# Experts taken by falling token count, with 448 to 384 columns, and an attention loop and tail arranged anew

## The chip, the core and the metric

The kernel runs on one core of a Trainium2 chip. A core has TensorE for matrix products, VectorE, ScalarE and GpSimd for work on elements, and SyncE, which issues most of the transfers between main memory and the core's memory (SBUF); products land in PSUM, an accumulator memory of eight banks. The engines run side by side, each through its own list of instructions in order, and wait for each other by semaphores. In the profile they are PE, DVE, ACT, POOL and SP; PEld is the loading of weights into TensorE. The metric is the time of one execution on the device, in us. The rows of a trace come from one profiled execution.

## The reference, cut to what matters

```python
def attn(q, k, v, f_logit):              # 4 batches, 8 heads, 768 tokens, 48 wide
    f = 1 / (1 + exp(-f_logit))
    for t in range(768):                 # a state of 48x48 for each batch and head
        state = f[t][:, None] * state + outer(k[t], v[t])
        y[t] = q[t] @ state
def moe(x, emb, tau, w1, w2):            # x = y as 3072 tokens of 384; 8 experts, hidden 1024
    logits = normed(x) @ normed(emb).T / tau
    e = argmax(logits); g = softmax(logits)[e]
    out[token] = g * relu(x[token] @ w1[e]) @ w2[e]
def moe2(x, w_a, w_b, w_out):            # sister: 384 -> 1536 -> 384
    return ((x @ w_a) * (x @ w_b)) @ w_out
result = moe2(moe(attn(q, k, v, f_logit)))
```

## The kernel before

All work is cut so that TensorE has products of 128 rows. Products that need the accuracy of float32 are made of three matmuls each, of a high and a low half (the names end in h and l).

**Attention.** 24 groups g (6 chunks of 128 tokens for each of 4 batches), one loop over g with the stages of several groups interleaved by hand. For each g: ScalarE makes the gate F with a tanh and then `F*0.5+0.5` (gate_f, three groups ahead). VectorE makes Bt, a running product of F, with a scan whose second operand `pat` says where it starts anew, then the reciprocal `patr`, and then Rt, a second scan over F and patr (scan_b, scan_r); `qc = q*Rt` (q_scale), and GpSimd `kt = k*Bt`. TensorE multiplies qc and kt (scores, tile pp), ScalarE, VectorE and GpSimd mask the product (pm; GpSimd's share is an affine select), TensorE forms y from pm and v and from the state S, and turns y to tokens (x_ps). VectorE updates S. Scan patterns and gates lie in SBUF. After groups 4, 8, 12, 16, 20 and 23 the tokens are routed (route, a generator that tick moves on): VectorE finds each token's expert from logits (mx, z, eq, m, oh), TensorE counts places (rk), VectorE makes the slot (pz, posi), and GpSimd scatters the token's row to a table `slots` in main memory, one transfer for each 128 tokens (scatter_row).

**Tail of attention.** The first EN = 224 tokens of expert 0 are computed early, beside the last routing (early_turn, early_h, early_split, early_y, late_turn), with weights w made from raw by w_hi and w_lo. Near its end the matmuls `pc` bring the token counts (run, run_e) and the least gate product (amp) to one row, pcs.

**Experts.** The tokens of expert e are CAP = 448 rows of `slots` (expert 0 has 224 left here). rows_load loads them, x_turn transposes them by TensorE (tile pt), and 8 steps s follow: h_part, 9 matmuls ph with the columns of all tokens, then y_part, 9 matmuls po. hh and hl are the two halves of relu(ph), made by ScalarE and VectorE; y_part of a step runs behind h_part of the next. At the end of an expert po is copied to yT at an offset off, a register read from the counts, so that rows of the next expert overwrite what is not filled. w_load and w_more bring the weights in 32 pieces of 768 KB, two of w1 and two of w2 for each expert, with a fixed order. If an expert has more tokens than CAP, a flag sends the kernel through a slower general path.

**Sister.** 72 steps of 18 matmuls with 512 columns and 12 with 384 (L1088 on), then the rows are scattered to the output.

Of the kernel before, what the change touches and what calls it, by code (L numbers as in the profile page):

```python
# [43 lines left out]
EN = 224  # L44
C0 = 2.0 ** -15


def build(tc, I, out, dbg=None):
# [28 lines left out]
    off_f = epool.tile([1, 4, NE], F32, name="off_f")  # L77
    fl2 = epool.tile([1, 4], F32, name="fl2")

    pieces = []  # L80
    w1, w2 = I["moe_w1"], I["moe_w2"]
    for e in range(NE):
        for s in range(2):
            pieces.append(w1[e].rearrange("(k p) f -> p k f", p=128)[:, :, s * 512:(s + 1) * 512])
            pieces.append(w2[e].rearrange("(j p) d -> p j d", p=128)[:, s * 4:(s + 1) * 4, :])
# [14 lines left out]
    def w_load():  # L100
        n = wstate["load"]
        if n >= NP1 or n - wstate["lo"] // 3 >= 2:
            return
        wstate["load"] += 1
        src = pieces[n]
        RAW[n] = raw_tile()
        SP.dma_start(out=RAW[n].rearrange("p (k f) -> p k f", k=src.shape[1]), in_=src)
# [19 lines left out]
    with tc.manual_schedule():  # L127
# [8 lines left out]
        ps_p = actx.enter_context(tc.tile_pool(name="ps_p", bufs=3, space=PSUM))  # L136
# [3 lines left out]
        ps_r = actx.enter_context(tc.tile_pool(name="ps_r", bufs=1, space=PSUM))  # L140
# [6 lines left out]
        pat = ob_p.tile([QP, NP, L + 1], F32, name="pat")  # L147
# [6 lines left out]
        patr_t = [ob_p.tile([QP, NP, L + 1], F32, name=f"patr{i}") for i in range(2)]  # L154
# [39 lines left out]
        def scan_b(g):  # L194
# [8 lines left out]
            V.reciprocal(out=patr_t[g % 2][:, :, 0], in_=Bt[:, :, 0])  # L203

        def scan_r(g):
# [4 lines left out]
            V.tensor_tensor_scan(out=fl(Rt), data0=Fx[g % 2][:, 0:n1], data1=fl(patr_t[g % 2]), initial=0.0,  # L210
# [150 lines left out]
        def route(rd):  # L361
# [26 lines left out]
            ps = ps_r.tile([128, RB, NE], F32, tag="r", name="rk")[:, 0:nb]  # L388
# [23 lines left out]
        def rows_load(e):  # L412
            at = EN if e == 0 else 0
            src = slots[e * NT + at:e * NT + CAP].rearrange("(p j) w -> p j w", p=HP)
            ld = SP.dma_start(out=rows_of(e)[0:HP, 2 if e == 0 else 0:4], in_=src).ins
# [148 lines left out]
        en_ps = ps_r.tile([128, NE], F32, tag="r", name="en_ps")  # L564
# [32 lines left out]
        for g in range(NG):  # L597
            it[0] = g
            load_a(g + 4)
# [6 lines left out]
            if g in (2, 10, 11, 17, 23):  # L606
                w_load()
            if g == 21:
                early_load()
# [12 lines left out]
            mask_v(g + 1)  # L622
            gate_f(g + 3)
# [16 lines left out]
            for _ in range(2 if len(scaled) > 3 or g >= 19 else 1):  # L640
                scatter_row()
# [8 lines left out]
            if g in (4, 5, 6, 12, 13, 14, 19, 20, 21):  # L650
# [17 lines left out]
            if g == 3:  # L668
                G.iota(out=xb_all[:, :, 0].rearrange("p (c b) -> p c b", b=B), pattern=[[L, NCH], [S, B]], base=0,
# [56 lines left out]
        for i in range(2):  # L726
            G.iota(out=off_f[:, 2 + i], pattern=[[CAP, NE]], base=0 if i else NT - NE * CAP, channel_multiplier=0,
                   allow_small_or_imprecise_dtypes=True)
        amp = ob_p.tile([128, 1], F32, name="amp")
        V.tensor_reduce(out=amp, in_=al_all, axis=AX.XY, op=ALU.min)  # L730
        early_split(5)
        early_y(4)
        pc = ps_r.tile([128, 2, 128], F32, tag="r", name="pc")
        T.transpose(pc[0:1, 1], amp, ident)
        T.matmul(out=pc[0:1, 0, 0:NE], lhsT=ones[:, 0:1], rhs=run, start=True, stop=True)
        T.matmul(out=pc[0:1, 0, NE:2 * NE], lhsT=ones[:, 0:1], rhs=run_e, start=True, stop=True)
        early_h(6)
        early_split(6)
        V.tensor_copy(pcs[:, 0, 0:2 * NE], pc[0:1, 0, 0:2 * NE])
        V.tensor_copy(pcs[:, 1], pc[0:1, 1])  # L740
# [15 lines left out]
        yT = [sp.tile([128, NT + CAP], F32, name=f"yT{k}") for k in range(KC)]  # L756
# [32 lines left out]
        def job_load(s):  # L789
            while jobs and len(loaded) < 2:  # L790
                n, c = jobs.pop()
                raw = raw_tile()
                src = pieces[n]
# [77 lines left out]
        def counts():  # L871
            cnt_sb = pcs[:, 0, 0:NE]
# [508 lines left out]
```

## Time and profile before

| | |
|---|---|
| median of 3 runs | 860.79 us (860.08 to 860.92) |
| profiled execution | 861.15 us, its span 859.4 us |
| TensorE busy | 832.4 us of the span (97%), mean granted clock 0.988 |
| VectorE, ScalarE, GpSimd busy | 410.5, 343.0, 225.4 us |
| start and first attention groups | 0 to 36.77 us |
| attention, 15 iterations | 36.77 to 119.18 us |
| attention, last iterations | 119.18 to 143.70 us |
| early work of expert 0, last routing | 143.70 to 168.67 us |
| rest of expert 0 | 168.67 to 184.93 us |
| experts 1 to 7 | 184.93 to 397.83 us |
| sister | 397.83 to 859.40 us |

The span runs from the first to the last instruction of the trace; the execution's own time has some 1.8 us around it. A stage's time is the difference of its ends; what TensorE is busy in it says whether it computes or waits. [...]

### The profile page before, as it was taken

What the parts mean: (1) busy time and instruction counts of PE and PEld (TensorE: products, weight loads), DVE (VectorE), ACT (ScalarE), POOL (GpSimd) and SP (SyncE); (2) the same over time, 40 slices, a digit from 0 to 9 for tenths busy, and PEclk for the clock granted to TensorE, in tenths of its full rate; (3) what the DMA queues carried; (4) which work ended last, traced back from release to release, by engine and by line L of the source; (5) the groups of instructions that cost most, each with busy time, mean ns of one, the idle gap of its engine ahead of it and who ended that gap; (6) DMA issues with size and microseconds to landing.
All of it is one profiled execution on the core that took longest, in us unless ns stands there. A gap on an engine that the chain in (4) does not pass through costs nothing.

```text
span 859.4 us, 12900 instructions
## 1 busy us (share of the span) xinstructions
PE 832.4 (97%) x5156; PEld 736.0 (86%) x5156; DVE 410.5 (48%) x684; ACT 343.0 (40%) x657; POOL 225.4 (26%) x194
## 2 busy tenths in 40 slices
PE   6999997999999999999999999999999999999996
PEld 4888886999899999998888888888888888888885
DVE  8999996355554544456886222221322222132222
ACT  4898885254454444444443212221221222122121
POOL 7457675143446444523000100100010010001001
PEclk8999999899999999999999999999999999999999
DMA  9989763354555356334240100000000000001001
GB/s 182 249 225 245 209 177 120 110 153 142 150 179 182 113 148 209 113 84 142 77 143 3 38 1 0 19 19 1 1 37 1 1 19 19 0 1 37 1 1 39
DMA packets 38667, 77.15 MB, mean 90 GB/s; under 512 B 7595, under 2 KB 20505, under 8 KB 38601
## 3 DMA queue, kind: packets, MB, share of 16 engines
q1 hardware_dynamic: 35401, 66.40, 28.0%
q0 software_dynamic: 3072, 9.56, 3.1%
q8 instruction: 42, 0.69, 0.3%
q10 hardware_dynamic: 128, 0.30, 0.1%
q14 instruction: 24, 0.20, 0.1%
HBM read 63.98 MB, written 12.26 MB: 89 GB/s over the span
## 4 chain that ended last, share of the span: by engine, by line
issue 61%; PE 17%; POOL 9%; DMA 6%; DVE 4%; ACT 1%; POOLq 0%; ACTq 0%; DVEq 0%
DMA raw<-moe_w 5%; PE po L978 3%; POOL w L817 3%; PE pp L253 2%; POOL out L1145 2%; POOL w L836 2%; DVE Rt L210 2%; PE y_ps L287 2%; PE x_ps L321 1%; PE y_ps L280 1%; PE ph L937 1%; PE ph L935 1%; PE ph L936 1%; PE kv L488 1%; DVE qc L218 1%
## 5 line engine op out<-in xcount | busy, mean ns | idle before, releaser
L936 PE MATMUL pa<-a,w 128*128 128x512 f32 (+1 forms) x438 | 172.0, 393 | 0.0
L937 PE MATMUL pa<-a,w 128*128 128x512 f32 (+1 forms) x438 | 171.1, 391 | 0.0
L935 PE MATMUL pa<-a,w 128*128 128x512 f32 (+1 forms) x438 | 171.0, 390 | 0.0
L1115 DVE TENSOR_TENSOR rows<-rows,pa 128x512 f32<-128x512 f32 (+1 forms) x73 | 49.6, 679 | 243.1 <-PE pa L937 227.0
L1145 POOL DMA_INDIRECT out<-yT,idx x24 | 23.4, 976 | 430.9 <-ACT yT L1143 425.5
L1109 ACT ACTIVATE rows<-pa 128x512 f32<-128x512 f32 (+1 forms) x73 | 43.3, 593 | 169.1 <-PE pa L937 169.0
L1116 ACT ACTIVATE gh<-rows 128x512 fp32r<-128x512 f32 (+1 forms) x73 | 45.8, 627 | 152.8 <-DVE rows L1115 150.1
L937 PEld LDWEIGHTS pa<-a,w 128*128 128x128 f32 x438 | 82.2, 188 | 18.9
L1131 PE MATMUL pq<-w,gh 128*128 128x384 f32 x288 | 96.3, 334 | 0.0
L935 PEld LDWEIGHTS pa<-a,w 128*128 128x128 f32 x438 | 82.1, 187 | 16.5
L1132 PE MATMUL pq<-w,gl 128*128 128x384 f32 x288 | 96.3, 334 | 0.0
L1130 PE MATMUL pq<-w,gh 128*128 128x384 f32 x288 | 96.3, 334 | 0.0
L936 PEld LDWEIGHTS pa<-a,w 128*128 128x128 f32 x438 | 82.1, 187 | 15.7
L978 PE MATMUL po<-hh,w 128*128 128x448 f32 (+1 forms) x384 | 86.1, 359 | 0.4 <-ACT yT L996 0.4
L817 POOL TENSOR_TENSOR w<-raw,w 128x512 fp32r<-128x512 f32 x48 | 72.7, 1535 | 40.3 <-ACT w L814 40.3
L958 ACT ACTIVATE hh<-ph 128x448 fp32r<-128x448 f32 (+1 forms) x64 | 33.3, 521 | 111.3 <-PE ph L937 110.6
L959 DVE SCALAR_TENSOR_TENSOR hl<-ph,hh 128x448 fp32r<-128x448 f32 (+1 forms) x64 | 38.0, 594 | 73.6 <-ACT hh L958 73.6
L978 PEld LDWEIGHTS po<-hh,w 128*128 128x128 f32 x384 | 67.8, 189 | 5.7 <-ACT yT L996 1.0
L1119 DVE TENSOR_TENSOR gl<-rows,gh 128x512 fp32r<-128x512 f32 (+1 forms) x73 | 49.9, 684 | 45.1 <-ACT gh L1116 42.3
L935 PE MATMUL ph<-a,w 128*128 128x448 f32 (+1 forms) x192 | 68.4, 356 | 0.0
L937 PE MATMUL ph<-a,w 128*128 128x448 f32 (+1 forms) x192 | 68.2, 355 | 0.0
L936 PE MATMUL ph<-a,w 128*128 128x448 f32 (+1 forms) x192 | 68.1, 355 | 0.0
(216 smaller groups left out, 1361.5 us busy)
## 6 DMA issues: line engine op xcount, KB each, us to landing
raw<-moe_w SPq DMA_DIRECT2D x32, 768.0 KB
qkf<-qkf SPq DMA_DIRECT2D x44, 288.0 KB
vx<-vx SPq DMA_DIRECT2D x24, 192.0 KB
raw<-moe_w_a SPq DMA_DIRECT2D x6, 768.0 KB
raw<-moe_w_b SPq DMA_DIRECT2D x6, 768.0 KB
raw<-moe_w_out SPq DMA_DIRECT2D x6, 768.0 KB
rows<-slots SPq DMA_DIRECT2D x6, 689.5 KB
slots<-raw SPq DMA_DIRECT2D x8, 295.5 KB
```

Of the source, the lines that this page charges most:

```text
L817: (G if i < NPOOL else V).tensor_tensor(out=wt[:, 1, f], in0=raw[:, f], in1=wt[:, 0, f].bitcast(F32), op=ALU.subtract)
L935: T.matmul(out=out, lhsT=wh, rhs=xh, start=first, stop=False)
L936: T.matmul(out=out, lhsT=wl, rhs=xh, start=False, stop=False)
L937: T.matmul(out=out, lhsT=wh, rhs=xl, start=False, stop=last)
L978: T.matmul(out=OS[e][k], lhsT=w[:, j % 4, k * 128:(k + 1) * 128], rhs=x, start=(j == 0 and w is wh and x is hh), stop=(j == FJ - 1 and x i ...
L1109: A.activation(out=ab[:, r], in_=pa, func=ACTF.Copy)
L1115: V.tensor_tensor(out=ab[:, r], in0=ab[:, r], in1=pp[1], op=ALU.mult)
L1116: A.activation(out=gh[:, r], in_=ab[:, r], func=ACTF.Copy)
L1119: V.tensor_tensor(out=gl[:, r], in0=ab[:, r], in1=gh[:, r].bitcast(F32), op=ALU.subtract)
L1130: T.matmul(out=q, lhsT=gh[:, c], rhs=wh[:, f % 4], start=(f == 0), stop=False)
L1131: T.matmul(out=q, lhsT=gh[:, c], rhs=wl[:, f % 4], start=False, stop=False)
L1132: T.matmul(out=q, lhsT=gl[:, c], rhs=wh[:, f % 4], start=False, stop=(f == F2J - 1))
```

## The change

Experts 1 to 7 are computed in the order of falling token count, and the place in that order, not the expert's number, sets how many columns are computed: CAPS. The order is found on the chip by VectorE in small operations (key, won, place_f, ord_i, srt) between the early products, from counts that pc now brings earlier. SyncE reads the place in main memory of weights and rows from ord_i. Limits for offsets are 24 constants (lims), set by GpSimd. Weight piece 4 is loaded behind rows_load(0), no longer at g = 23, and piece 5 behind the rows of expert 1.

In the attention, pat and patr move from SBUF to two banks of PSUM (resets), one patr instead of two. For it ps_p has two buffers instead of three, rk lies in the bank of u_ps and pc in a tile of x_ps. gate_f goes to GpSimd from g = 3 on. Where a routing is under way, pz and posi are made ahead of the scans (tick(2) behind mask_v), so that scatters start an iteration earlier; the two extra scatters at g = 19 are gone. Several loads and conversions move by one iteration.

```diff
+CAPS = (CAP, 448, 432, 416, 408, 400, 392, 384)
...
+            place[e] = [SP.value_load(ord_i[0:1, i, e:e + 1], min_val=a, max_val=(NE - 1) * a)
+                        for i, a in enumerate((DM, FF))] if e else (0, 0)
...
+            rows_e = I["moe_w1"].rearrange("e r f -> (e r) f")[bass.ds(at, DM) if e else slice(0, DM)]
...
-        ps_p = actx.enter_context(tc.tile_pool(name="ps_p", bufs=3, space=PSUM))
+        ps_s = actx.enter_context(tc.tile_pool(name="ps_s", bufs=1, space=PSUM))
+        ps_p = actx.enter_context(tc.tile_pool(name="ps_p", bufs=2, space=PSUM))
...
-        ps_r = actx.enter_context(tc.tile_pool(name="ps_r", bufs=1, space=PSUM))
...
-        pat = ob_p.tile([QP, NP, L + 1], F32, name="pat")
+        resets = ps_s.tile([128, 1024], F32, name="resets")
+        patr = resets[:, 0:NP * (L + 1)].rearrange("p (a b) -> p a b", a=NP)
+        pat = resets[:, (NP - 1) * (L + 1) + 1:(2 * NP - 1) * (L + 1) + 1].rearrange("p (a b) -> p a b", a=NP)
...
+        u_bank = ps_u.tile([128, 512], F32, name="u_ps")
...
+        r_ps = u_bank[:, NP * HP:NP * HP + RB * NE]
...
-                A.activation(out=F[:, :, 0:L], in_=F[:, :, 0:L], func=ACTF.Copy, scale=0.5, bias=0.5)
+                if g < 3:
+                    A.activation(out=F[:, :, 0:L], in_=F[:, :, 0:L], func=ACTF.Copy, scale=0.5, bias=0.5)
+                else:
+                    G.tensor_scalar(out=F[:, :, 0:L], in0=F[:, :, 0:L], scalar1=0.5, scalar2=0.5,
+                                    op0=ALU.mult, op1=ALU.add)
...
-            ps = ps_r.tile([128, RB, NE], F32, tag="r", name="rk")[:, 0:nb]
+            ps = r_ps.rearrange("p (b e) -> p b e", b=RB)[:, 0:nb]
...
+                at = SP.value_load(ord_i[0:1, 2, e:e + 1], min_val=NT, max_val=(NE - 1) * NT)
+                src = slots[bass.ds(at, CAPS[e])].rearrange("(p j) w -> p j w", j=4)
...
-            if g in (2, 10, 11, 17, 23):
+            if g in (2, 10, 11, 17):
                 w_load()
...
             mask_v(g + 1)
+            if fresh and g < NG - 1:
+                tick(2)
...
+                for e in range(NE):
+                    for i, v in enumerate((max(0, NT - sum(CAPS[e:])), min(NT, sum(CAPS[0:e])), CAPS[e])):
+                        G.memset(lims[:, i, e:e + 1], float(v))
...
         early_h(0)
+        bg.append(route(dict(rd, n=3)))
+        tick(6)
         early_split(0)
         x_copy(NG - 1, rd)
         x_sq(NG - 1, rd)
-        rd["n"] = 3
-        bg.append(route(rd))
-        tick(6)
         early_h(1)
...
         tick(3)
+        amp = ob_p.tile([128, 1], F32, name="amp")
+        V.tensor_reduce(out=amp, in_=al_all, axis=AX.XY, op=ALU.min)
...
+        T.matmul(out=pc[0][0:1, 0:NE], lhsT=ones[:, 0:1], rhs=run, start=True, stop=True)
+        T.matmul(out=pc[0][0:1, NE:2 * NE], lhsT=ones[:, 0:1], rhs=run_e, start=True, stop=True)
+        T.transpose(pc[1][0:1], amp, ident)
         early_h(2)
+        V.tensor_copy(pcs[:, 0, 0:2 * NE], pc[0][0:1, 0:2 * NE])
         w_hi(1)
         early_split(2)
+        key, won, place_f = (ob_p.tile([1, 7, 7], F32, name=nm) for nm in ("key", "won", "place_f"))
...
+        V.tensor_tensor(out=won, in0=key[:, 0].unsqueeze(2).to_broadcast(big), in1=key[:, 0].unsqueeze(1).to_broadcast(big),
+                        op=ALU.is_ge)
...
         def n_of(e):
-            return CAP - EN if e == 0 else CAP
+            return CAP - EN if e == 0 else CAPS[e]
...
-                        dst = yT[k][:, bass.ds(off, CAP)]
+                        dst = yT[k][:, bass.ds(off, CAPS[e])]
```

GpSimd's order in the attention, two iterations before. kt is k times Bt, pm the masked scores, the DMA row the scatter of 128 tokens.

```order
L427 DMA slots<-xb,posi 24576x394
L202 TENSOR_TENSOR kt<-qkf_142,Bt 128x512
L264 AFFINE_SELECT pm_1055<-pm_1055 128x512
L427 DMA slots<-xb,posi 24576x394
L202 TENSOR_TENSOR kt<-qkf_143,Bt 128x512
L264 AFFINE_SELECT pm_1149<-pm_1149 128x512
```

The same place of the changed kernel:

```order
L226 TENSOR_TENSOR kt<-qkf_143,Bt 128x512
L288 AFFINE_SELECT pm_1082<-pm_1082 128x512
L212 TENSOR_SCALAR F_142<-F_142 128x4x128
L456 DMA slots<-xb,posi 24576x394
L226 TENSOR_TENSOR kt<-qkf_144,Bt 128x512
L288 AFFINE_SELECT pm_1175<-pm_1175 128x512
L212 TENSOR_SCALAR F_141<-F_141 128x4x128
```

One instruction more stands in each iteration, behind the affine select and ahead of the scatter; Bt of the next iteration needs it.

VectorE's order in the tail before: he is the low half of the first early product in u_ps, mx to oh are the routing of the last tokens.

```order
L477 SCALAR_TENSOR_TENSOR he_152<-u_ps,he_151 128x224
L374 TENSOR_REDUCE mx<-xb 128x3
L377 TENSOR_TENSOR z<-xb,mx 128x24
L380 SCALAR_TENSOR_TENSOR eq<-z,prio 128x24
L383 TENSOR_REDUCE m_2127<-eq 128x3
L386 TENSOR_TENSOR oh<-eq,m_2127 128x24
L477 SCALAR_TENSOR_TENSOR he_154<-y_ps,he_153 128x224
```

The same place of the changed kernel:

```order
L375 TENSOR_REDUCE xb<-pp 128x8
L398 TENSOR_REDUCE mx<-xb 128x3
L401 TENSOR_TENSOR z<-xb,mx 128x24
L404 SCALAR_TENSOR_TENSOR eq<-z,prio 128x24
L407 TENSOR_REDUCE m_2138<-eq 128x3
L410 TENSOR_TENSOR oh<-eq,m_2138 128x24
L506 SCALAR_TENSOR_TENSOR he_153<-u_ps,he_152 128x224
L506 SCALAR_TENSOR_TENSOR he_155<-y_ps,he_154 128x224
```

The routing, up to oh, now stands ahead of he of u_ps; the matmuls that read oh write to u_ps's bank.

TensorE's order there before: the end of early_y(0), then early_h(2) (u_ps) and early_y(1).

```order
L488 MATMUL kv<-he_151,w_65 128x224 x2
L488 MATMUL pq<-he_151,w_65 128x224
L488 MATMUL kv<-he_152,w_65 128x224 x2
L488 MATMUL pq<-he_152,w_65 128x224
L472 MATMUL u_ps<-a_85,w_64 128x224 x9
L488 MATMUL kv<-he_153,w_65 128x224 x2
```

The same place of the changed kernel, with pc between the two:

```order
L517 MATMUL pq<-he_152,w_65 128x224
L517 MATMUL kv<-he_153,w_65 128x224 x2
L517 MATMUL pq<-he_153,w_65 128x224
L743 LDWEIGHTS ones
L743 MATMUL pc<-run,ones 1x8
L744 LDWEIGHTS ones
L744 MATMUL pc<-run_e,ones 1x8
L745 MATMUL pc<-ident,amp 1x128
L501 MATMUL u_ps<-a_85,w_64 128x224 x9
L517 MATMUL kv<-he_154,w_65 128x224 x2
```

The three products pc, which stood behind early_y(4), now wait on this place for run, run_e and amp of VectorE, and early_h(2) is queued behind them.

TensorE's order at the change from expert 1 to expert 2 before: the last po of expert 1, then the first ph of expert 2.

```order
L978 MATMUL po<-hh,w_65 128x448 x6
L978 MATMUL po<-hl,w_65 128x448 x3
L935 MATMUL ph<-a_2377,w_66 128x448
L936 MATMUL ph<-a_2377,w_66 128x448
L937 MATMUL ph<-a_85,w_66 128x448
```

The same place of the changed kernel:

```order
L1026 MATMUL po<-hh,w_65 128x448 x6
L1026 MATMUL po<-hl,w_65 128x448 x3
L983 MATMUL ph<-a_2423,w_66 128x432
L984 MATMUL ph<-a_2423,w_66 128x432
L985 MATMUL ph<-a_85,w_66 128x432
```

The order of the matmuls is the same; those of the second expert in the new order have 432 columns, and so on down to 384.

## Rows read from the trace of the kernel before

**Rows 1.** Page, part 1: busy time, share of the span, instructions.
```profile
PE 832.4 (97%) x5156; PEld 736.0 (86%) x5156; DVE 410.5 (48%) x684; ACT 343.0 (40%) x657; POOL 225.4 (26%) x194
```

**Rows 2.** Table by stretch: length, busy time by engine (count), clock, DMA share, GB/s.
```profile
36.77:119.18 82.41, 78.42 (x1040) 68.26 (x1040) 80.62 (x141) 72.13 (x190) 52.22 (x43) 1.00 0.89 230
...
143.70:168.67 24.97, 22.33 (x175) 21.76 (x173) 8.96 (x32) 7.74 (x23) 6.02 (x8) 0.86 0.32 104
168.67:184.93 16.26, 16.26 (x150) 16.26 (x148) 9.74 (x31) 9.48 (x22) 8.77 (x9) 1.00 0.62 179
184.93:397.83 212.90, 212.50 (x1084) 194.98 (x1082) 104.89 (x154) 96.11 (x138) 94.74 (x60) 1.00 0.48 145
```

**Rows 3.** Chain of waits in experts 0 and 1: start, us, what.
```profile
182.07 1.00 PE po L978 x9
...
184.09 1.00 PE po L978 x9
...
189.79 1.82 PE po L978 x9
...
193.46 1.82 PE po L978 x9
...
197.13 0.39 PE pt L925 x4
```

**Rows 4.** Timeline of TensorE, two attention iterations: start, us, line, operation.
```profile
41.87 1.16 PE L253 MATMUL pp<-qc,kt 64*128 64x128 f32 x16
...
46.98 1.16 PE L253 MATMUL pp<-qc,kt 64*128 64x128 f32 x16
```

**Rows 5.** Table by stretch, the score matmuls (L253) alone.
```profile
36.77:119.18 82.41, 17.43 (x241) 14.85 (x241) 1.00 0.89 230
119.18:136.28 17.10, 3.48 (x48) 2.97 (x48) 1.00 0.30 97
```

**Rows 6.** Timeline of VectorE, two attention iterations.
```profile
91.38 1.22 DVE L199 TENSOR_TENSOR_SCAN Bt<-F,pat 128x516 f32<-128x516 f32 x1
...
93.95 1.22 DVE L210 TENSOR_TENSOR_SCAN Rt<-F,patr 128x516 f32<-128x516 f32 x1
95.21 0.94 DVE L218 TENSOR_TENSOR qc<-qkf,Rt 128x512 f32<-128x512 f32 x1
...
100.24 1.65 DVE L210 TENSOR_TENSOR_SCAN Rt<-F,patr 128x516 f32<-128x516 f32 x1
101.92 0.69 DVE L218 TENSOR_TENSOR qc<-qkf,Rt 128x512 f32<-128x512 f32 x1
```

**Rows 7.** Groups of VectorE, 36.77 to 136.28: busy us, mean ns, idle before.
```profile
L210 DVE TENSOR_TENSOR_SCAN Rt<-F,patr 128x516 f32<-128x516 f32 x18 | 27.8, 1546 | 0.0
...
L273 DVE TENSOR_TENSOR pm<-pp,mask 128x512 f32<-128x512 f32 x18 | 12.3, 684 | 0.0
...
L122 DVE TENSOR_TENSOR w<-raw,w 128x512 fp32r<-128x512 f32 x6 | 4.1, 680 | 0.0
```

**Rows 8.** Waits of ScalarE, 168 to 200: total us, times, longest.
```profile
ACT w L807 <- DMA raw<-moe_w: 1.4, 2, 0.9
```

**Rows 9.** Timeline around the last routing: start, us, engine, line [idle before].
```profile
148.74 0.39 DVE L477 SCALAR_TENSOR_TENSOR he<-u_ps,he 128x224 fp32r<-128x224 f32 x1 [2.42 <-ACT he L476]
...
149.90 0.18 DVE L386 TENSOR_TENSOR oh<-eq,m 128x24 bf16<-128x24 f32 x1
...
150.13 0.20 PE L389 MATMUL rk<-oh,tri 128*128 128x24 bf16 x1 [2.64 <-DVE oh L386]
```

**Rows 10.** Groups of GpSimd, 0 to 150: busy us, mean ns, idle before.
```profile
L202 POOL TENSOR_TENSOR kt<-qkf,Bt 128x512 f32<-128x512 f32 x24 | 29.7, 1239 | 36.6 <-PE pp L253 9.9 <-issue 8.7 <-DVE Bt L199 7.2
L264 POOL TENSOR_SCALAR_AFFINE_SELECT pm<-pm 128x512 f32<-128x512 f32 x23 | 21.8, 948 | 1.4 <-ACT pm L263 1.0
...
L585 POOL TENSOR_TENSOR en<-en,half 128x8 f32<-128x8 f32 x1 | 2.6, 2593 | 2.4 <-ACT en L582 2.4
```

**Rows 11.** Table by stretch, one of three alike up to 156.
```profile
150.00:152.00 2.00, 1.86 (x12) 1.81 (x13) 0.99 (x6) 0.32 (x1) 0.12 (x1) 0.50 0.03 8
```

More of the change, by code (lines that the diff above doesn't have):

```diff
@@ L76, in build, with piece @@
     pcs = epool.tile([1, 2, 128], F32, name="pcs")
-    off_f = epool.tile([1, 4, NE], F32, name="off_f")
+    off_f = epool.tile([1, 2, NE], F32, name="off_f")
+    lims = epool.tile([1, 3, NE], F32, name="lims")
+    srt = epool.tile([1, 2, NE], F32, name="srt")
+    ord_i = epool.tile([1, 3, NE], I32, name="ord_i")
     fl2 = epool.tile([1, 4], F32, name="fl2")
[L80 to L85, printed above, removed]
+    pieces = [None] * 4 * NE
+    place = {}
+    def piece(n):
+        if pieces[n] is not None:
+            return pieces[n]
+        e, r = divmod(n, 4)
+        if e not in place:
+            place[e] = [SP.value_load(ord_i[0:1, i, e:e + 1], min_val=a, max_val=(NE - 1) * a)
+                        for i, a in enumerate((DM, FF))] if e else (0, 0)
+        s, i = divmod(r, 2)
+        at = place[e][i]
+        if i == 0:
+            rows_e = I["moe_w1"].rearrange("e r f -> (e r) f")[bass.ds(at, DM) if e else slice(0, DM)]
+            return rows_e.rearrange("(k p) f -> p k f", p=128)[:, :, s * 512:(s + 1) * 512]
+        rows_e = I["moe_w2"].rearrange("e r d -> (e r) d")[bass.ds(at, FF) if e else slice(0, FF)]
+        return rows_e.rearrange("(j p) d -> p j d", p=128)[:, s * 4:(s + 1) * 4, :]
     for s in range(3):
@@ L104, in w_load @@
         wstate["load"] += 1
-        src = pieces[n]
+        src = piece(n)
         RAW[n] = raw_tile()
@@ L202, in scan_b @@
             G.tensor_tensor(out=kt, in0=d["qkf"][:, 1], in1=Bt[:, :, 1:L + 1], op=ALU.mult)
-            V.reciprocal(out=patr_t[g % 2][:, :, 0], in_=Bt[:, :, 0])
+            V.reciprocal(out=patr[:, :, 0], in_=Bt[:, :, 0])
         def scan_r(g):
@@ L538, in build @@
             V.memset(F[:, n1:], 0.0)
+        V.memset(patr, 0.0)
         V.memset(pat, 0.0)
@@ L639, in build @@
                 turn_y(g - 1)
-            for _ in range(2 if len(scaled) > 3 or g >= 19 else 1):
+            for _ in range(2 if len(scaled) > 3 or g >= 20 else 1):
                 scatter_row()
@@ L715, in build @@
         early_split(3)
+        V.tensor_tensor(out=won, in0=place_f, in1=pcs[:, 0, 1:NE].unsqueeze(1).to_broadcast(big), op=ALU.mult)
+        V.tensor_reduce(out=srt[:, 0, 1:NE], in_=won, axis=AX.X, op=ALU.add)
+        V.tensor_copy(srt[:, 0, 0:1], pcs[:, 0, 0:1])
         early_y(2)
@@ L725, in build @@
         early_h(5)
[L726 to L730, printed above, removed]
         early_split(5)
         early_y(4)
[L733 to L736, printed above, removed]
         early_h(6)
         early_split(6)
-        V.tensor_copy(pcs[:, 0, 0:2 * NE], pc[0:1, 0, 0:2 * NE])
-        V.tensor_copy(pcs[:, 1], pc[0:1, 1])
+        V.tensor_copy(pcs[:, 1], pc[1][0:1])
         early_y(5)
@@ L755, in build @@
         sp = ectx.enter_context(tc.tile_pool(name="solo", bufs=1))
-        yT = [sp.tile([128, NT + CAP], F32, name=f"yT{k}") for k in range(KC)]
+        yT = [sp.tile([128, max(sum(CAPS), NT + DM)], F32, name=f"yT{k}") for k in range(KC)]
         rows1 = yT[2][:, NT - 4 * RW:NT].rearrange("p (j w) -> p j w", j=4)
@@ L792, in job_load @@
                 raw = raw_tile()
-                src = pieces[n]
+                src = piece(n)
                 if c is None:
@@ L895, in off_range @@
         def off_range(e):
-            return dict(min_val=max(0, NT - (NE - e) * CAP), max_val=min(NT, e * CAP))
+            return dict(min_val=max(0, NT - sum(CAPS[e:])), max_val=min(NT, sum(CAPS[0:e])))
         def rows_load_n(e):
@@ L908, in ids_store @@
                 rs = SP.value_load(off_i[0:1, e:e + 1], **off_range(e))
-                dst = heads[bass.ds(rs, CAP)]
+                dst = heads[bass.ds(rs, CAPS[e])]
             n = 2 if e == 0 else 4
-            SP.dma_start(out=dst.rearrange("(p j) w -> p j w", j=n), in_=ids[e % 2][:, 0:n])
+            SP.dma_start(out=dst.rearrange("(p j) w -> p j w", j=n), in_=ids[e % 2][0:n_of(e) // n, 0:n])
         def ids_copy(e):
```

64 lines of the change are left out of this document (39 added, 25 removed).

## The prediction

> **What bounds the kernel now.** I read the page first: TensorE is busy for 97% of the span [rows 1], so the question for every edit is whether it shortens TensorE's own work, or a wait in front of it. Then I cut the span into its stages [rows 2]. In experts 1 to 7 TensorE is busy 212.50 of 212.90 us: that stage is a sum of matmuls and nothing else. In the attention iterations from 36.77 to 119.18 it is busy 78.42 of 82.41 us, and VectorE 80.62 of the same 82.41: two engines that are both nearly full, so either may be late in an iteration. In the stretch from 143.70 to 168.67 TensorE has 2.6 us of gaps and a mean granted clock of 0.86.
>
> For the experts the chain of waits gives the price of a step [rows 3]. Two neighbouring groups of po matmuls stand 193.46 − 189.79 = 3.67 us apart at 448 columns (9 ph and 9 po matmuls), and 184.09 − 182.07 = 2.02 us apart at 224. So time does follow the columns: (3.67 − 2.02) / (18 × 224) = 0.41 ns for a column of a matmul, with some 20 ns that are there at any width.
>
> For the attention the timeline of TensorE shows the iteration when nothing is late: scores at 41.87 and again at 46.98, 5.11 us [rows 4]. Each iteration has 16 score matmuls, so the 241 counted from 36.77 to 119.18 are 15 iterations [rows 5], and 15 × 5.11 = 76.65 us: 5.8 us of the 82.41 are excess. The next three iterations, of the last chunk, take 17.10 us [rows 5]; some of TensorE's work is gone there, so VectorE's own chain is their floor.
>
> That chain is in the timeline of VectorE [rows 6]. From Bt's scan to Rt's scan is 2.57 us (93.95 − 91.38), Rt's scan keeps the engine 1.26 us (95.21 − 93.95) and qc some 0.6 where it is short: about 4.5 us. But the same scan Rt is 1.22 us at 93.95 and 1.65 us at 100.24, and qc 0.94 and 0.69. The mean of Rt over these 18 iterations is 1.546 us [rows 7], where the scan Bt, of the same shape, is never long. The long ones stand beside reads by GpSimd.
>
> **The change, part by part.** *Narrower experts.* 7 × 448 = 3136 columns become 448 + 432 + 416 + 408 + 400 + 392 + 384 = 2880. Of 256 columns each passes 18 matmuls in 8 steps: 36,864 × 0.41 ns = **−15.2 us**. The transposes pt take 0.39 us for four of 112 columns [rows 3]; over the 84 of them 768 columns go (12 for each expert, a quarter of 256 in sum), at (0.39/4 − 0.02)/112 = 0.7 ns: **−0.5**. I bound this term by −14.5 and −16.2. TensorE waits for nothing there, so the whole of it comes off the end, as long as what feeds it (weights, hh and hl) keeps up. The columns of hh and hl shrink as well.
>
> *Weights at an address read on the chip.* SyncE reads the order out of ord_i before each expert's loads, two registers for weights and one for rows. Before has the same kind of read ahead of its heads writes. The load of piece 4 was issued in attention and piece 5 ahead of the two row loads; now they come behind rows_load(0) and behind one row load. In 168:200 ScalarE already waits 1.4 us for raw weights, 0.9 the longest [rows 8], while TensorE was busy 16.26 of 16.26 us [rows 2]. What hides it is that hh is ready a step early; without that cover a load later by 2 us would cost up to 2 us. I take **0**, bounds 0 and +2.
>
> *The sort.* Thirteen VectorE operations on 1x7 or 1x49, with none of that size in a row; the nearest are small operations such as oh, 0.18 us [rows 9], so about 2.4 us. VectorE is busy 8.96 of 24.97 us in that stretch [rows 2]; I take 0, bounds 0 and +1. The 24 one-element memsets of GpSimd fall in one early iteration: between nothing and 24 × 0.18 = 4.3 us of GpSimd once (by the same row), of which an iteration leaves free 5.11 − 3.48 = 1.63 (3.48 below), so 0 to +1.
>
> *Reset patterns in PSUM.* The scans Bt and Rt now read one operand from SBUF and one from PSUM. What an operand in PSUM costs VectorE shows at pm, which reads pp from PSUM and the mask from SBUF, against w, which reads two from SBUF: 0.684 and 0.680 us [rows 7]. So nothing is paid, and I expect Rt at 1.22 wherever it stands. [...] The pair of rows differs by 4 ns, and the sum goes by it. In the iterations with excess VectorE is the late engine, so 18 × (1.546 − 1.22) = 5.9 us of VectorE's time go. Not all reaches TensorE, which has only 5.8 us to lose over the 15. A route iteration adds five small operations (about 1.05 us) behind qc, the next one four (0.7), and some carry a w of 0.68; with a plain chain of 4.5 against 5.11 these are made up within one or two iterations. I take **−4** for the 15, bounds 0 and −5.8; **−2.5** for the three behind them (17.10 against 3 × 4.5 = 13.5, so 0 to −3.6); and **−0.5** for the first three (bounds 0 and −0.8, by the same price for a scan).
>
> [...]
>
> *The gate on GpSimd.* F·0.5 + 0.5, one ScalarE instruction an iteration, goes to GpSimd. ScalarE was busy 72.13 of 82.41 us [rows 2] with VectorE above it at 80.62; I count nothing for its relief. No row of GpSimd has this form at this size: below it the affine select over 128x512, one read, 0.948 us in the mean; above it kt, two reads, 1.239; far above pow, 2.593 us on 128x8 [rows 10]. I take 0.95, as the form is nearest to the affine select. GpSimd is busy 52.22 us over 15 iterations [rows 2], 3.48 each, so 4.4 of 5.11 after; it stays off the path. But it reads SBUF for 0.95 us more, beside a qc that rises from 0.69 to 0.94 when GpSimd reads. That is why I do not take the whole 5.8.
>
> *Tail.* Before, TensorE idles 2.64 us up to 150.13 for oh, which is queued on VectorE behind he at 148.74 [rows 9]. Now the route comes ahead of the split: oh is ready some 0.8 us earlier, but its matmuls write in the bank of u_ps and so wait until he has read that: about −0.9 us. Against it, the matmuls of pc stand ahead of early_h(2) and wait for run and amp, two or three VectorE operations later than the route's matmuls (up to +1), and the two late transposes now share one PSUM bank, so the second waits for VectorE's read of the first (up to +1.1). The clock falls to 0.50 after this gap [rows 11] and stays there for three such stretches, so 6 us of work is half done and some 3 us are lost; if the shorter gap keeps the clock, they return. I take **−1**, bounds +2 and −4.
>
> **The sum.** The profiled execution took 861.15 us. −15.2 − 0.5 − 0.5 − 4 − 2.5 − 1 = −23.7: 837.45. It was 0.36 above the median of the runs, so I forecast a median of **837.1**.
>
> **The rivals.**
> 1. *The attention gives little* (0.17): the contention moves from Rt to qc and w, because GpSimd now reads for most of the iteration. For it: qc at 0.94, and GpSimd at 4.4 of 5.11. Against it: with Rt short, VectorE's plain chain has 0.6 us of room in each iteration, and a qc of 0.94 takes 0.25 of it. Then the experts and the tail alone: 861.15 − 15.7 − 1 = 844.4, median 844.
> 2. *More of it* (0.13): attention at its floor (−0.8 − 5.8 − 3.6 = −10.2) and a tail that keeps the clock (−3): 861.15 − 15.7 − 13.2 = 832.2, median 832.
> 3. *Experts stall* (0.02): an expert's first weights or rows arrive 1 us late because SyncE's reads hold its queue. 7 experts: +7 on the forecast, 844. Against it: raw is loaded many steps ahead later on.
> 4. *Narrow matmuls do not shorten* (0.02): the weight load of each matmul is the limit, so the change does not do what it says. Then −8 alone, 853. The pair at 224 columns excludes it nearly: 2.02 us for 18 is 112 ns each.
> 5. *Slower* (0.03): GpSimd becomes the bound. Iterations now take 82.41/15 = 5.49 us; to eat the 16.7 us of experts and tail over the 18 iterations they would have to take 5.49 + 0.93 = 6.42, so GpSimd's own 3.48 plus a gate of more than 2.94 us. At pow's 2.59 the iterations would be 6.07, 18 × 0.58 = 10 us up, 854; at 3.5 us, 6.98, 27 us up, 871. One row in sight (pow) comes near; the form speaks against it.
>
> The forecast has 0.62, no change 0.01. Its own range is 834 to 841; with most of rivals 1 and 2 the range is **832 to 844.5**. A measurement of this kernel can tell some 0.2% from no change (1.7 us). Faster: 0.62 + 0.17 + 0.13 + 0.02 + 0.02 = 0.96; same 0.01; slower 0.03.
>
> **What would show it.** Right: po groups at 384 columns 18 × 64 × 0.41 = 0.47 us closer than at 448, and an expert stage of about 197 us with no wait of TensorE over 0.5; every Rt at 1.22; scores 5.11 apart in most iterations; the gate at about 0.95 on GpSimd. Wrong: Rt or Bt above 1.25 everywhere (the PSUM operand has a price), qc at 0.94 or more in most iterations, scores waiting for kt (GpSimd late), ScalarE waiting over 2 us for raw in expert 0 with TensorE behind it, or a clock of 0.50 longer than 6 us behind 150.

## The result, and the profile after

The changed kernel took 836.31 us (median of 4 runs, 833.71 to 838.48), the kernel before 860.55 beside it: a ratio of 0.9717, 95% interval 0.9689 to 0.9746. Run again beside other kernels it gave 837.59 us and 0.9733 (0.9715 to 0.9751). The profiled execution was the fastest of its runs (833.71, span 832.0), so the sizes below are read with a second profile of the same kernel beside it (e0, below; 838.45, span 836.8). Of the kernel before there is one profile.

The table by stretch of the changed kernel, as in [rows 2], for the 15 iterations, the early work with the last routing, experts 1 to 7, and the rest of expert 0:

```profile
33.88:113.53 79.65, 77.80 (x1040) 68.07 (x1040) 77.20 (x144) 65.14 (x174) 52.02 (x61) 1.00 0.95 250
...
136.63:157.28 20.65, 17.95 (x159) 17.34 (x159) 9.92 (x40) 6.69 (x20) 5.29 (x5) 1.00 0.35 116
...
173.55:369.87 196.32, 195.81 (x1084) 190.09 (x1082) 99.62 (x154) 93.42 (x137) 94.95 (x59) 1.00 0.51 156
157.28:173.55 16.27, 16.27 (x150) 16.27 (x149) 9.75 (x31) 9.37 (x22) 8.73 (x9) 1.00 0.71 214
```

Set against the landmarks of before (first scores, scores of the iterations, first early product, first product of the experts, first of the sister, end), this is where 27.4 us of the span went, and 22.6 in the second profile:

| stretch | before, us | after, us | second profile, us | forecast of the change |
|---|---|---|---|---|
| to the first scores | 10.08 | 9.28 | 9.33 | none |
| first five iterations | 26.68 | 24.61 | 25.26 | −0.5 |
| 15 iterations | 82.41 | 79.64 | 80.03 | −4 |
| next three | 17.10 | 14.16 | 14.16 | −2.5 |
| to the first early product | 8.94 | 8.94 | 8.94 | none |
| early work, last routing | 23.44 | 20.66 | 22.45 | −1 |
| experts | 229.16 | 212.58 | 214.29 | −15.7 |
| sister to the end | 461.56 | 462.14 | 462.30 | none |

The groups of VectorE in the changed kernel from 33.88 to 127.69, the same 18 iterations as in [rows 7]:

```profile
L223 DVE TENSOR_TENSOR_SCAN Bt<-F,resets 128x516 f32<-128x516 f32 x18 | 22.0, 1221 | 0.5 <-POOL F L212 0.5
L234 DVE TENSOR_TENSOR_SCAN Rt<-F,resets 128x516 f32<-128x516 f32 x18 | 21.9, 1219 | 0.0
L242 DVE TENSOR_TENSOR qc<-qkf,Rt 128x512 f32<-128x512 f32 x18 | 14.7, 818 | 0.6
```

Rt's mean fell from 1546 to 1219 ns; every scan is now as long as the short ones were. qc's mean did not change (818 before and after), but one of the 18 now takes 2.17 us (e4, below), and the other 17 have 738 ns. The groups of GpSimd, beside [rows 10]:

```profile
L226 POOL TENSOR_TENSOR kt<-qkf,Bt 128x512 f32<-128x512 f32 x24 | 28.4, 1183 | 29.2 <-PE u_ps L325 11.7 <-PE u_ps L418 6.9 <-PE pp L277 6.2
...
L288 POOL TENSOR_SCALAR_AFFINE_SELECT pm<-pm 128x512 f32<-128x512 f32 x23 | 15.1, 656 | 2.3 <-ACT pm L287 2.2
L212 POOL TENSOR_SCALAR F<-F 128x512 f32<-128x512 f32 x21 | 13.4, 640 | 0.0
```

The gate takes 0.640 us there, and the affine select fell from 948 to 656 ns: the scans had been slowing GpSimd as well. GpSimd does 21 gates more and is no busier, 222.6 us in all for 225.4.

The chain of waits in expert 7 (384 columns), as in [rows 3]:

```profile
352.52 1.57 PE po L1026 x9
...
355.64 1.57 PE po L1026 x9
```

3.12 us a step against 3.67 at 448.

### The profile page after: what moved, and what is told of

It reads as the page before. It is cut to its first block, busy times and chain, and to the rows that moved or that the text cites. A ratio compares the mean times of both kernels' runs of the same rounds, so it can differ in the third digit from the quotient of the medians.

```text
span 832.0 us, 13075 instructions
## 1 busy us (share of the span) xinstructions
PE 812.0 (98%) x5156; PEld 728.0 (88%) x5156; DVE 398.1 (48%) x696; ACT 331.1 (40%) x636; POOL 222.6 (27%) x237
## 4 chain that ended last, share of the span: by engine, by line
issue 54%; PE 31%; DVE 7%; POOL 3%; DMA 2%; ACT 2%; POOLq 0%; SPq 0%; ACTq 0%; DVEq 0%
PE po L1026 11%; PE ph L983 4%; PE ph L985 4%; PE ph L984 4%; POOL out L1193 2%; DVE Rt L234 2%; PE pp L277 2%; PE x_ps L345 1%; PE y_ps L304 1%; PE y_ps L311 1%; DVE qc L242 1%; DVE Bt L223 1%; DMA vx<-vx 1%; PE pt L973 1%; DVE pm L297 1%
## 5 line engine op out<-in xcount | busy, mean ns | idle before, releaser
L1026 PE MATMUL po<-hh,w 128*128 128x224 f32 (+7 forms) x384 | 81.0, 345 | 0.5 <-ACT yT L1044 0.5
L983 PE MATMUL ph<-a,w 128*128 128x224 f32 (+7 forms) x192 | 65.5, 341 | 0.0
L985 PE MATMUL ph<-a,w 128*128 128x224 f32 (+7 forms) x192 | 65.3, 340 | 0.0
L984 PE MATMUL ph<-a,w 128*128 128x224 f32 (+7 forms) x192 | 65.3, 340 | 0.0
L1006 ACT ACTIVATE hh<-ph 128x224 fp32r<-128x224 f32 (+7 forms) x64 | 31.5, 492 | 81.0 <-PE ph L985 80.9
L1007 DVE SCALAR_TENSOR_TENSOR hl<-ph,hh 128x224 fp32r<-128x224 f32 (+7 forms) x64 | 35.8, 560 | 45.7 <-ACT hh L1006 45.3
```

Of the source, the lines that this page charges most:

```text
L983: T.matmul(out=out, lhsT=wh, rhs=xh, start=first, stop=False)
L984: T.matmul(out=out, lhsT=wl, rhs=xh, start=False, stop=False)
L985: T.matmul(out=out, lhsT=wh, rhs=xl, start=False, stop=last)
L1026: T.matmul(out=OS[e][k], lhsT=w[:, j % 4, k * 128:(k + 1) * 128], rhs=x, start=(j == 0 and w is wh and x is hh), stop=(j == FJ - 1 and x i ...
```

## The experiments

Comparisons go by the ratio to the kernel before on the same chip: beside e1, e2, e3 and e5 it took 857.59 us, beside the others 860.5 to 860.6.

**e1, the columns put back.**

```diff
-CAPS = (CAP, 448, 432, 416, 408, 400, 392, 384)
+CAPS = (CAP,) * 7 + (432,)
...
-        yT = [sp.tile([128, max(sum(CAPS), NT + DM)], F32, name=f"yT{k}") for k in range(KC)]
+        yT = [sp.tile([128, NT + CAPS[7]], F32, name=f"yT{k}") for k in range(KC)]
```

> The changed kernel with experts 1 to 6 at 448 columns and the last at 432, so 240 of the 256 removed columns are back; sort, order and all else stay. Theory (the expert term is the columns alone): the stretch from the first product of the experts to the first of the sister grows from 212.6 to about 228 us (15 to 16 us up), the attention and the tail stay, time about 852. Rival (the new order, the reads of addresses or the weights' later issue carry part of the change): the stretch differs from the 229.2 us of the kernel before by over 2 us after the 1 us for the 16 columns that stay out.

850.69 us, ratio 0.9906 (0.9873 to 0.9938). The experts, table by stretch:

```profile
158.03:386.19 228.16, 227.69 (x1231) 211.11 (x1229) 113.87 (x185) 105.22 (x159) 103.69 (x69) 1.00 0.50 151
```

15.6 us longer than the changed kernel's 212.6, and 1.0 under the 229.2 of before, which is what 16 columns are worth. In this profile the reads of addresses and the later weights cost the experts nothing that can be seen; the gain there is columns alone.

**e2, the patterns back in SBUF; e3, the gate back on ScalarE; e8, both back.**

```diff
-        ps_s = actx.enter_context(tc.tile_pool(name="ps_s", bufs=1, space=PSUM))
...
-        resets = ps_s.tile([128, 1024], F32, name="resets")
+        resets = ob_p.tile([128, 1024], F32, name="resets")
```

```diff
-                if g < 3:
+                if g < NG:
                     A.activation(out=F[:, :, 0:L], in_=F[:, :, 0:L], func=ACTF.Copy, scale=0.5, bias=0.5)
```

> The changed kernel with the reset patterns of both scans back in SBUF (one copy, as in the changed kernel), the gate still on GpSimd. Theory (contention of the scan Rt with reads of GpSimd is what the attention lost before): Rt's mean back at 1.5 us or more, the affine select back from 0.66 to 0.9 us, the attention up to the early products 6 to 10 us longer, time 842 to 847. Rival (the gain came from ScalarE's relief and the order of the small operations): under 3 us longer.

> The changed kernel with the gate F back on ScalarE in every iteration. Theory (the gate on GpSimd costs nothing and gains little, ScalarE was not late): attention within 1 us. Rival 1 (the gate's reads on GpSimd are what makes qc long): qc's mean falls from 0.82 to about 0.72 and the iteration of 6.85 us shrinks, 1 to 2 us less. Rival 2 (ScalarE is late with 0.63 us more): 2 us or more longer, with TensorE waiting for ktT, pm or S.

> The changed kernel with the patterns back in SBUF and the gate back on ScalarE, the fourth corner with the changed kernel, the patterns alone back and the gate alone back. The first group's scores to the first early product took 127.4 us in the changed kernel, 143.1 with the patterns back, 126.5 with the gate back, 135.2 before. Theory (the gate on GpSimd costs little only because the scans no longer contend): about 134 us, so that the gate's move by itself costs some 9 us with patterns in SBUF and under 1 with them in PSUM; time about 839. Rival (the two effects add): 142 us, time 847.

e2 took 848.33 us (0.9883, 0.9865 to 0.9901), e3 831.49 (0.9686, 0.9668 to 0.9704), e8 841.63 (0.9777, 0.9761 to 0.9793). From the first scores to the first early product, in the traces:

| | gate on GpSimd | gate on ScalarE |
|---|---|---|
| patterns in PSUM | 127.35 and 128.39 us | 126.52 us (e3) |
| patterns in SBUF | 143.05 us (e2) | 133.65 us (e8; before: 135.14) |

The groups of VectorE in e2, 38.42 to 144.21:

```profile
L233 DVE TENSOR_TENSOR_SCAN Rt<-F,resets 128x516 f32<-128x516 f32 x18 | 30.6, 1702 | 0.0
L222 DVE TENSOR_TENSOR_SCAN Bt<-F,resets 128x516 f32<-128x516 f32 x18 | 22.1, 1226 | 2.5 <-POOL F L211 2.5
```

And of GpSimd in e2, 0 to 155:

```profile
L211 POOL TENSOR_SCALAR F<-F 128x512 f32<-128x512 f32 x21 | 28.3, 1346 | 0.0
L287 POOL TENSOR_SCALAR_AFFINE_SELECT pm<-pm 128x512 f32<-128x512 f32 x23 | 21.0, 913 | 0.5 <-ACT pm L286 0.4
```

e2 lost 15 us where I expected 6 to 10, and its time lies above the 842 to 847 that I gave, because the gate itself is in the contention: 1.346 us for 0.640, Rt at 1.702, and Bt waits for the gate. The effects do not add. Moving the patterns is worth 7 us with the gate on ScalarE and 15 with it on GpSimd; moving the gate costs 9.4 us with the patterns in SBUF and 0.8 to 1.9 with them in PSUM. That last difference is small against the spread: the same attention takes 128.5 to 129.7 us in the profiles of e1, e5 and e11, and the time of e3 lies 1.6 us under that of e5 beside it (the changed kernel with a small Relu ahead of time, below), with intervals that overlap. So the gate's move is a loss with the patterns in SBUF and no gain that can be seen with them in PSUM. qc in e3 is shorter, 30 to 135 us (811 ns in the changed kernel there):

```profile
L242 DVE TENSOR_TENSOR qc<-qkf,Rt 128x512 f32<-128x512 f32 x19 | 14.2, 750 | 0.6
```

That is the mechanism of my first rival, at a small part of its price. e8's attention came out as its theory had it (133.65 for about 134 us); its time did not (841.63 for about 839), and its early work has a fall of the clock in it (22.08 us). The 1.5 us between e8 and before, one profile each, are what is left for the rest of the new arrangement of the attention.

**e4, the scatters split.** The one iteration that got worse is the second behind the first routing: 6.85 us (6.14 before). The timelines of GpSimd and VectorE in the changed kernel show what stands there:

```profile
58.08 0.98 POOL L456 DMA_INDIRECT slots<-xb,posi  x1 [0.30 <-ACT S L248]
...
59.06 1.21 POOL L226 TENSOR_TENSOR kt<-qkf,Bt 128x512 f32<-128x512 f32 x1
...
59.24 2.17 DVE L242 TENSOR_TENSOR qc<-qkf,Rt 128x512 f32<-128x512 f32 x1
...
60.19 0.66 POOL L288 TENSOR_SCALAR_AFFINE_SELECT pm<-pm 128x512 f32<-128x512 f32 x1
...
60.80 1.08 POOL L212 TENSOR_SCALAR F<-F 128x512 f32<-128x512 f32 x1
...
61.56 1.16 PE L277 MATMUL pp<-qc,kt 64*128 64x128 f32 x16 [1.68 <-DVE qc L242]
```

Two scatters hold kt back, so that three reads by GpSimd fall beside one qc, which takes 2.17 us for 0.69, and TensorE waits 1.68.

```diff
-            for _ in range(2 if len(scaled) > 3 or g >= 20 else 1):
+            for _ in range(2 if 3 < len(scaled) < 5 or g >= 20 else 1):
```

> The changed kernel, but where five scatters stand ready (behind the first routing alone) GpSimd issues one in that iteration and two in the next, in place of two and one. Theory (two scatters make kt late there, so that kt, the affine select and the gate all read SBUF beside one qc, which takes 2.17 us for 0.69): that qc falls below 1.2 us, the iteration of 6.85 us to 5.5 or less, and with the gap the falls of the clock behind it; 1 to 2 us less, and 2 us less spread. Rival (VectorE's small routing operations make that iteration late, the long qc only fills a wait): under 0.5 us.

835.42 us, 0.9712 (0.9696 to 0.9728), against e0's 0.9733 (0.9715 to 0.9751) on the same chip. In its trace that qc, of VectorE's timeline, is short again:

```profile
59.51 0.69 DVE L242 TENSOR_TENSOR qc<-qkf,Rt 128x512 f32<-128x512 f32 x1
```

The iteration takes 5.37 us (7.17 in e0), so the collision is shown as what made it long. The 1.8 us in the medians fit, but the intervals overlap, and the runs lie no closer together (834.29 to 836.73) than e0's (836.84 to 839.36): that part of the expectation was wrong.

The split does not always remove it. Of the five profiles with it (e4, e10, e12, e13, e14) one, e13, has the collision again, with the gate on ScalarE. By the timelines of GpSimd and VectorE the first scatter starts late, and qc takes 2.03 us:

```profile
58.64 1.24 POOL L457 DMA_INDIRECT slots<-xb,posi  x1 [5.41 <-DMA qkf<-qkf]
59.91 1.19 POOL L226 TENSOR_TENSOR kt<-qkf,Bt 128x512 f32<-128x512 f32 x1
...
59.63 2.03 DVE L242 TENSOR_TENSOR qc<-qkf,Rt 128x512 f32<-128x512 f32 x1
```

TensorE waits 1.34 us there and the iteration takes 6.52. Without the split qc takes 1.78 to 2.49 us in the changed kernel's first profile, e0, e1 and e3; in e5 and e11 the scatters are later still, qc is short (0.69), and TensorE waits 1.3 to 1.4 us for kt. When the scatters start is therefore the open question, not only how many there are.

**e0, the changed kernel again.**

> The changed kernel once more, beside the next three on the same chip. Theory (its spread of 5 us comes from the clock after gaps of TensorE, one of 1.7 us in the iteration behind the first routing and one of 1.6 us ahead of the last): ratio near 0.972, again 3 us or more between its fastest and slowest run, and a profile in which each of the two gaps is or is not followed by a granted clock of 0.50.

Its spread is 2.5 us, not the 3 or more that I expected. Both gaps are there, of 2.00 and 1.75 us, and behind the second the granted clock, which the traces give as a share of full speed, falls to 0.50, in the table by stretch:

```profile
144.00:146.00 2.00, 2.00 (x12) 2.00 (x11) 0.06 (x1) 0.18 (x1) 1.70 (x2) 0.50 0.28 105
```

In the first profile of the same kernel it stays at 1.00 through that stage. So the early work took 20.66 us with a whole clock and 22.45 with the fall; e4 and e11, which have the same tail and the same fall, took 22.39 and 22.43. In e1 the clock fell behind the other gap, of 1.71 us ahead of 62.40:

```profile
64.00:66.00 2.00, 2.00 (x15) 1.74 (x15) 1.98 (x5) 1.43 (x6) 1.87 (x3) 0.50 1.05 224
```

and its next iteration took 6.72 us for 5.11. In these falls the clock is low for 3.4 us, and they cost 1.6 to 1.8; in e12 (below) it is low for 6.8, and that costs 2.9 against e10, which has the same gaps. The same gap may or may not bring a fall. How much of the spread that is can be estimated from the mean granted clock that is on record for each run: over the 60 runs of the changed kernel and its variants, each set against the mean of its own kernel, 0.001 less clock goes with 0.7 us more, and that accounts for a little over half of the variance. e4's spread stayed because its split takes away one gap of two; its profile has a fall behind the other.

**e5 and e11, a Relu of ScalarE ahead of time.** The gap ahead of the last routing comes from `he`, ScalarE's first Relu, which starts late behind its product:

```profile
136.63 1.26 PE L501 MATMUL u_ps<-a,w 128*128 128x224 f32 x9
...
139.65 0.36 ACT L505 ACTIVATE he<-u_ps 128x224 fp32r<-128x224 f32 x1 [2.45 <-PE y_ps L501]
...
140.48 0.17 PE L413 MATMUL u_ps<-oh,tri 128*128 128x24 bf16 x1 [1.59 <-DVE he L506]
```

```diff
         tick(30)
+        first = ob_p.tile([128, 1], F32, name="first")
+        A.activation(out=first, in_=half[:, 0:1], func=ACTF.Relu)
         for _ in range(4):
             scatter_row()
```

> The changed kernel with one extra Relu of ScalarE on one column of 128 rows, behind the last attention iteration, before ScalarE's first Relu he. In the trace he starts 1.76 us behind the end of its product in the kernel before and in the changed one. Theory (the first Relu pays some 1.3 to 1.7 us that no row shows, such as a change of function): he starts within 0.4 us of its product, TensorE's gap of 1.6 us ahead of the last routing falls below 0.5, time 1 to 1.5 us less, and less spread between runs. Rival (he waits for the second early product or for its queue): nothing moves.

> The changed kernel with the early Relu once more, beside a kernel without it on the same chip, since the four executions profiled in its first call had no gap ahead of he with or without it (0.04 us), and all others had one of 1.75 to 1.93 us. Theory (first Relu, on a chip or in executions where it costs): he starts 0.04 us behind its product here while the control e13 shows 1.8. Rival (the gap belongs to the chip or the placing of the program, not to Relu): both with the gap, or both without.

e5 took 833.07 us (0.9711, 0.9672 to 0.9749) and showed no gap, but nor did e1, which has no early Relu:

```profile
139.09 1.26 PE L501 MATMUL u_ps<-a,w 128*128 128x224 f32 x9
...
140.39 0.36 ACT L505 ACTIVATE he<-u_ps 128x224 fp32r<-128x224 f32 x1 [0.73 <-PE u_ps L501]
```

e11 (835.32 us, 0.9702, 0.9683 to 0.9721) has the Relu and the gap, 1.91 us behind the product:

```profile
135.93 0.19 ACT L711 ACTIVATE first<-half 128x1 f32<-128x1 f32 x1
...
140.99 0.36 ACT L505 ACTIVATE he<-u_ps 128x224 fp32r<-128x224 f32 x1 [2.55 <-PE y_ps L501]
```

The theory fell. Over all 14 profiles the gap is 0.04 us in the four that ran together on one chip (e1, e2, e3, e5) and 1.75 to 1.93 in the ten others, before's among them. It is nothing of the change, and its cause stays open. The clock fell in the early work of seven of the ten (not in the changed kernel's first profile, e10 and e14) and in none of the four.

**e10, e13, e12 and e14, the gaps taken together.** e10 and its repeat e13 have the edits of e3 and e4 and these, which give the second late transpose and the last routing's counts the bank of the scan patterns; e12 adds the Relu, and e14 to that puts the pc products behind early_h(2).

```diff
-            pp = [ps_p.tile([128, 512], F32, tag="pp", name="pl") for _ in range(2)]
+            pp = [ps_p.tile([128, 512], F32, tag="pp", name="pl"), resets[:, 512:1024]]
...
-            ps = r_ps.rearrange("p (b e) -> p b e", b=RB)[:, 0:nb]
+            last = resets[:, 512:512 + RB * NE] if nb == 3 else r_ps
+            ps = last.rearrange("p (b e) -> p b e", b=RB)[:, 0:nb]
```

> The changed kernel with the gate back on ScalarE, the scatters split as in e4, the second late transpose in the free bank of the scan patterns, and the last routing's counts in that bank too, so that they don't wait for VectorE's read of u_ps. Theory (these are the three gaps that are left): no wait of TensorE over 1 us between 40 and 160 us, the stretch from the first early product to the experts 1 us shorter than 18.9, attention 1 us shorter than 126.5, time 828 to 830, spread under 2 us. Rival (the waits move to qc and he): within 0.3% of the gate alone back (831.5).

> e10 again, the control of e11, e12 and e14: ratio to before near 0.9685; whether he has its gap of 1.8 us decides what the other three can show.

> e10 with the early Relu. By the theory of e11 the stretch from the first early product to the experts falls from 19.55 to about 18 us where the control has the gap, and time is 1 to 2 us under e13; by its rival the two are equal within 0.15%.

> e12 with the products pc behind early_h(2) in place of ahead of it. In e10 TensorE waits 0.8 us at pc for run. Theory (the pc products' place costs the tail that wait): no wait at pc, 0.5 to 0.8 us less than e12. Rival (the order of the experts then comes later and the weights with it): TensorE stalls in expert 0, or no change.

e10 took 833.20 us (0.9685, 0.9664 to 0.9706), e13 831.23 (0.9665, 0.9647 to 0.9683), e12 833.12 (0.9682, 0.9663 to 0.9701), e14 830.29 (0.9662, 0.9638 to 0.9686). The waits of TensorE in e14, 13 to 160 us:

```profile
PE pp L277 <- DVE qc L242: 2.6, 5, 1.3
PE kv L518 <- ACT he L506: 0.9, 1, 0.9
PE pp L277 <- ACT pm L287: 0.6, 1, 0.6
PE pp L277 <- DVE half L696: 0.2, 1, 0.2
```

The waits at pl (1.0 us) and at the routing (1.6) are gone in all four. In the place of the second, the next product kv waits 0.8 to 0.9 for `he`. The wait of 0.8 at pc stays in e10, e12 and e13 and is gone in e14. e10's stage of early work took 19.55 us, not the 17.9 expected, with these two waits in it; e14's took 18.62, and with the clock fallen e13's took 21.02 and e12's 22.49, so that the Relu gained nothing. e10 has no wait over 1 us between 40 and 160 us, as expected, but its repeat e13 has the 1.34 of the collision; e10's time and its spread of 4.9 us lie above the 828 to 830 and the 2 us that I gave. All four lie some 4 to 6 us under e0 by the ratio, with intervals apart from e0's. On the chip of e12, e13 and e14, however, e11 is the changed kernel with the Relu alone, and they lie 1.7 to 3.4 us under it, with intervals that touch or overlap. Which of the four is best, and whether they beat the gate alone (e3, on the chip without the gap of `he`), the intervals don't tell.

## Why the prediction was right, by its steps

**Experts, −15.7: −16.6 in the profile** (−14.9 in the second, which lost 1.3 us in the rest of expert 0, below). The mechanism and the place were right; the price of a column, 0.41 ns, was a little low. Steps of 384 and 448 that wait for nothing differ by 3.67 − 3.12 = 0.55 us, 0.48 ns for a column, and from 224 to 384 it is (3.12 − 2.02) / (18 × 160) = 0.38: the line is bent, and the removed columns lie on its steep part. Over the whole stage, with the transposes at the predicted 0.5 us, it comes to (16.6 − 0.5) / 36,864 = 0.44 ns.

**Weights and sort at 0** held in the first profile only. ScalarE's waits for raw weights in expert 0, 157 to 190 us, grew from 1.4 [rows 8] to 2.8 us:

```profile
ACT w L853 <- DMA raw<-moe_w: 2.8, 3, 1.3
```

and TensorE was busy 16.27 of 16.27 us there: the cover was enough. In e0, the same kernel, they are 6.0 us, 160 to 193:

```profile
ACT w L853 <- DMA raw<-moe_w: 6.0, 3, 2.7
...
160.17:177.75 17.58, 16.89 (x149) 16.44 (x148) 9.64 (x32) 9.21 (x22) 8.28 (x9) 1.00 0.68 205
```

The rest of expert 0 took 17.58 us there, 1.3 more (the second line, by stretch). That is the sign of being wrong that the prediction named, ScalarE waiting over 2 us for raw with TensorE behind it. ScalarE stands 2.7 us before one piece, and what it makes behind it for the transposes comes late, so that TensorE waits 0.6 us there. Of the 13 profiles of the changed kernel and its variants six have 16.3 us in this stage and seven 16.5 to 17.6, so the term was 0 to 1.3 us, inside its bounds. That the later issue of the loads makes it is not shown, since before has one profile; and no run has the sort alone.

**Patterns in PSUM at no price** held: Bt, which was never long before either, takes 1221 ns with the PSUM operand and took 1225 in the same 18 iterations of before. That a scan with one operand in PSUM would also be clear of GpSimd's reads, which the 1.22 of the forecast took for granted, was assumed: no row of before shows it. The runs do. In the changed kernel all 18 scans Rt of these iterations have an affine select, a gate or a kt of GpSimd running beside them for a part of their time, and each takes 1.22 us; in e3 their mean is 1.218. With both inputs in SBUF it is 1.63 in e8, and 1.70 in e2, where GpSimd has the gate as well.

One reading of the prediction was wrong here: that the long Rt, 1.65 us, are the ones with reads by GpSimd beside them, and those of 1.22 not. In GpSimd's timeline of before an affine select stands beside both scans of [rows 6]:

```profile
94.06 1.54 POOL L264 TENSOR_SCALAR_AFFINE_SELECT pm<-pm 128x512 f32<-128x512 f32 x1
...
100.17 0.63 POOL L264 TENSOR_SCALAR_AFFINE_SELECT pm<-pm 128x512 f32<-128x512 f32 x1
```

The Rt of 93.95 began 0.11 us ahead of one, kept its 1.22, and the affine select took 1.54 for 0.63; the Rt of 100.24 began 0.07 us behind one, which kept its 0.63, and Rt took 1.65. Of the 18 scans Rt in those iterations, 13 began while a read by GpSimd ran and took 1.64 to 1.76 us, three began ahead of one and took 1.22 while GpSimd's took 1.44 to 1.54, one stood alone, and one doesn't fit (49.27: 0.07 us behind, and yet 1.22). So in 16 of these 18 it was the one that started second that was lengthened.

**Attention, −7: −7.8 in the profile, −6.7 in the second** (−8.6 and −7.5 with the stretch ahead of the first scores). The sum was right, two terms of it were not. The setup and the first five iterations gave 2.9 us (2.2 in the second profile), where I had 0.5 for three of them: the scans of the setup were in contention too, and the first Rt fell from 2.11 to 1.23 us. The clock, which the prediction left out, may have a part in it: between 11 and 24 us it is at 0.50 for 10.2 us in all three profiles with the patterns in SBUF (before, e2, e8) and for 6.8 in all eleven with them in PSUM. The 15 iterations gave 2.8 where I had 4: of their excess 3 us stay, 1.7 of it in the collision of e4, the rest beside the routings, where pz and posi now stand ahead of Rt (0.3 us).

**The gate at 0.95 us** was too dear: 0.640. I priced it by an affine select whose mean held the contention that the same change took away. That it brings nothing and lengthens qc a little was right; that it was harmless holds only with the patterns in PSUM.

**Tail, −1: −2.8 with the whole clock, −1.0 with the fall.** Both signs of what I weighed are there: the gap of 2.64 us is 1.59, pc waits 0.1 us and pl 1.0. What decides the size is the clock: three of the four profiles with this tail and the gap have the fall (e0, e4, e11) and give −1.0, so the −2.8 is the rarer case of the four. Without the gap the stage is 18.9 us (e1, e2, e3, e5), but before has no profile without it to set beside that.

**The total.** That the median (836.31) lies within 0.8 us of the forecast is in part luck: one profile lies 3.7 us under the sum of 837.45 and the other 1.0 over it, and what parts them most, a fall of the clock (1.8) and waits in expert 0 (1.3), differs between runs of the same kernel.

## What to carry to other kernels

Before pricing an instruction by a row, ask whether that row holds a contention that the change removes; the short and the long instances of one shape in the timeline tell. Two moves that bear on the same contention can be worth 7 us, 15 or −9 according to order, so test them in all four corners before keeping both. When two instructions contend, look at which started first before saying which of them pays. A price for columns is taken from two widths near those that change, not from a far one.

## What the runs showed of the hardware that was not expected

Contention of a scan with GpSimd raises both means in e2, Rt from 1.22 to 1.70 us, the gate from 0.64 to 1.35, the affine select from 0.66 to 0.91; in a single overlap it is mostly the one that started second that is lengthened (1.22 and 1.54, or 0.63 and 1.65, in before). A qc beside three such reads took 2.17 us for 0.69. The granted clock fell to 0.50 behind a gap of TensorE of 1.75 us in e0 and stayed at 1.00 behind one of 1.59 in the first profile of the same program, and behind one of 2.00 earlier in e0. And ScalarE's `he` starts either 0.04 or 1.75 to 1.93 us behind its product, by the chip or the time it ran and not by the kernel (e5 and e11 are the same). In the changed kernel's first profile VectorE read the product ahead of it (pp) 0.7 us late as well, which may point to TensorE's side, but no run settles it. The sister, which no edit touches, took 0.2 to 0.8 us more in all profiles than in the one of before.
